# A Fourier mixing and low-rank mixer kernel: where batch 0's narrow sums run, when batch 1 is folded, and how its sine groups are formed

## The chip, the cores and the metric

The kernel runs on one core of one Trainium2 chip. The time is device microseconds of one launch; lower is better. The kernel before was timed three times: 446.45, 447.03 and 447.28 us, median 447.03 us. Five engines work side by side, each through its own queue in order: TensorE (PE; its weight loads are the row PEld), VectorE (DVE), ScalarE (ACT), GpSimd (POOL) and SyncE (SP, which here only issues DMAs).

## The reference

The input `x` is 8 batches of 3136 rows of 256 channels. Each batch goes through a two-dimensional Fourier transform, of which the real part is kept; then a low-rank mixing along the rows is added, and then a two-layer product over the channels.

```python
X = np.fft.fft(x, axis=1)
X = np.fft.fft(X, axis=2)
x = X.real.astype(np.float32)              # 8 x 3136 x 256

xt = x.transpose(0, 2, 1)
h = xt @ U @ V                             # rank 32, along the 3136 rows
u = x + h.transpose(0, 2, 1)
ch = np.maximum(u @ w_ch1, 0.0) @ w_ch2    # 256 -> 1024 -> 256
out = u + ch
```

## The kernel before

The Fourier transforms are matrix products with tables of sines and cosines (`tabs`: 0 is sine, 1 is cosine) that the kernel generates itself. Real input and the symmetry of sines and cosines let it work on folded data: rows n and S-n, channels d and D-d, and the two halves of the rows are added and subtracted first.

**Fold (`fold`, L402).** For a batch `b`, rows arrive in `xf` (forward) and `xr` (reversed), two halves `a` each. For each half VectorE folds along the channels (`along_d`, L382, instruction at L386, two parts for each of `xr` and `xf`), then combines forward and reversed rows (`mirror`, L394, into `EOS`); at the end `half` (L398) combines the two halves into `G[b % 2][par]`, the stationary operand of the transform. In batch 1, GpSimd copies channel 0 aside (`alone`, L390). `load_half` (L106) issues the loads of the next batch through GpSimd's queue. These are 16 steps for batch 1.

**Transform along the rows (`seq`, L470).** For each `par` (parity of the output), `typ` (1 cosine, 0 sine) and `pn` (parity of the row tile) there is a group of four products of 128 x 425 columns into one PSUM bank of the tag `dft`, of which there are three. The group with `pn == 0` is copied out by ScalarE (`ev`, L489); with `pn == 1`, VectorE forms the sum of both (`up`, L500) and their difference (`down`, L504) into the arrays `A` (cosine) and `B` (sine), and the small sum `TF` (L492) for the low-rank part. For some groups the `pn == 0` half is itself folded at the output: `halves` (L425) computes only the 229 columns from the middle on, in two parts, and VectorE forms the other columns from their difference (L436) and these from their sum (L437). `quarters` does the same twice, for the batches from `B0 = 2` on.

**The narrow row (`first_channel`, L614, through `narrow`, L545).** The first channels of batches 0 and 1 need a product of their own with 32 stationary columns: 16 small products into `ptc` (L556), a copy by ScalarE of one half of the partitions to `evc` (L560), and three operations for each parity on a few partitions: the small sum (L570), `up` (L573) and `down` (L574) into row R of `VA[b]`, the moving operand of the low-rank product. VectorE can read the other half of `ptc` in PSUM. Where `eng` is GpSimd, ScalarE also copies that half to `evo` (L563), and the sums read both from SBUF. Batch 1 and the later batches' shared narrow step use GpSimd; batch 0 uses VectorE. With `late` given, the two `down` operations are handed back and run later.

**Channels and the chunks.** `chan` (L628; `even_ch` and `odd_ch` for later batches) transforms pieces of `A` and `B` along the channels into `S` and `T`. The rows of all batches are then worked on in 49 chunks of 512 rows. `front(c)` (L712) forms a chunk's `u`: a low-rank product (L709) into PSUM, and VectorE's sum of it with `S` or `T` (L725). `first_product` (L729, product at L735) multiplies with `w_ch1`, ScalarE applies the maximum with 0 (L737); `second_product` (L739, product at L751) multiplies with `w_ch2`, and VectorE adds `u` (L757 to L760).

**What sets the order.** The setup, batch 0 and the first chunk are written in the order in which each engine's queue runs them (`tc.manual_schedule()`). At the start of chunk 1 (`c == 1`) `order.close()` ends that; from there on a planner orders the instructions by priority, which follows the program's order, and by its own estimate of when each is ready. Only those marked by `pin` keep the program's order. The loop of chunks has eight slots each (slot 8c + j). The dictionary `due` holds what else is issued in a slot; `spread(steps, lo, hi)` puts step n of N at slot `lo + (hi - lo) * n // N`:

```python
        for j in range(JT):
            if c < NCH:
                first_product(c, j)
            if c > 0 and j % 2 == 1:
                second_product(c - 1, j // 2)
            for step in due.get(8 * c + j, []):
                step()
            if j == 3 and c + 1 < NCH:
                front(c + 1)
```

So what is due in slot 3 stands ahead of `front(1)`, in slot 11 ahead of `front(2)` and in slot 19 ahead of `front(3)`. The pieces of batch 0's channels that are left are due in slots 2, 3, 8, 9, 10 and 11, behind the first two pieces and the late `down`s. Behind those, GpSimd's queue has its fills (`ta_rows(1)`, `column_zeros`, `ME`, `g_zeros(1)`, `va_zeros(1)`, L986 to L991), then what the fold issues.

Of the kernel before, what the change touches and what calls it, by code (L numbers as in the profile page):

```python
# [27 lines left out]
def kernel(  # L28
# [9 lines left out]
    nc = tc.nc  # L38
# [67 lines left out]
    def load_half(b, a):  # L106
        load_f(b, a)
        load_r(b, a)
        load_0(b, a, nc.gpsimd)
# [177 lines left out]
    def ktiles(par):  # L287
        return [i for i in range(NI) if (i + 1) % 2 == par]

    def kp(i):  # L290
        return KP if i == NI - 1 else PQ
# [90 lines left out]
    def along_d(a, src, dst, part):  # L382
        v = src[:, a, :, P:]
        lo, hi = (bass.AP(v.tensor, v.offset, [v.ap[0], v.ap[1], [s, 2], [2 * s, QD]])
                  for s in (-1, 1))
        pin(nc.vector.tensor_tensor(  # L386
            dst[:, a, :, part * P:(part + 1) * P].rearrange("p i (k t) -> p i k t", k=2), lo, hi,
            op=AL.subtract if part == 0 else AL.add))

    def alone(a, src, dst):  # L390

        pin(nc.gpsimd.tensor_copy(dst[:, a, :, 256:257], src[:, a, :, 0:1]))

    def mirror(a, cols, op):  # L394
        pin(nc.vector.tensor_tensor(EOS[:, a, :, cols], EOF_[:, a, :, cols],  # L395
                                    EOR_[:, a, ::-1][:, :, cols], op=op))

    def half(b, par, cols):  # L398
        pin(nc.vector.tensor_tensor(G[b % 2][par][:, :, cols], EOS[:, 0, :, cols],  # L399
                                    EOS[:, 1, :, cols], op=AL.add if par == 0 else AL.subtract))  # L400

    def fold(b):  # L402

        for a in range(2):
            for src, dst in ((xr, EOR_), (xf, EOF_)) if b == 1 else ((xf, EOF_), (xr, EOR_)):
                if b < B0:
                    yield lambda a=a, src=src, dst=dst: (alone(a, src, dst),
                                                         along_d(a, src, dst, 0))
                else:
                    yield lambda a=a, src=src, dst=dst: along_d(a, src, dst, 0)  # L410
                yield lambda a=a, src=src, dst=dst: along_d(a, src, dst, 1)
            if b + 1 < B:
                yield lambda a=a: load_half(b + 1, a)
            yield lambda a=a: mirror(a, slice(0, 128), AL.subtract)
            yield lambda a=a: mirror(a, slice(128, 258 if b < B0 else 256), AL.add)
        for par in range(2):
            yield lambda par=par: half(b, par, slice(0, 258 if b < B0 else 256))
# [48 lines left out]
    def join_t(eng):  # L466

        eng.tensor_tensor(TS, TF[:, :, 0], TF[:, :, 1], op=AL.add)  # L468

    def seq(b, par, typ, pn):  # L470

        if b not in ST:
            d = ST[b] = {}
            d["A"] = wp.tile([P, HALF + 1], BF16, tag="A", name="A", bufs=1)
            d["B"] = wp.tile([P, HALF + 1], BF16, tag="B", name="B", bufs=1)
            d["S"] = wp.tile([P, HALF + 1], BF16, tag="S", name="S", bufs=2)
            d["T"] = wp.tile([P, HALF + 1], BF16, tag="T", name="T", bufs=2)
        d = ST[b]
        g = G[b % 2][par]
        if pn == 0 and (b >= B0 or b == 1 and typ == 1):  # L480
            (quarters if b >= B0 else halves)(d, g, par, typ)
            return
        pt = psum.tile([P, QW], FP32, tag="dft", name="pt", bufs=3)
        for n, i in enumerate(ktiles(pn)):
            nc.tensor.matmul(pt[:], g[:kp(i), i, P * typ:P * (typ + 1)], tabs[typ][:kp(i), i, par, :],  # L485
                             start=(n == 0), stop=(n == NI // 2 - 1))
        if pn == 0:
            ev = d["ev"] = wp.tile([P, QW], FP32, tag="ev", name="ev", bufs=4)
            nc.scalar.copy(ev[:], pt[:])  # L489
            return  # L490
        ev = d["ev"]
        nc.vector.tensor_tensor(TF[:, typ, par], pt[:, NQ:QW], ev[:, NQ:QW], op=AL.add)  # L492
        if b == 0 and typ == 1 and par == 1:
            join_t(nc.vector)
        dst = d["A"] if typ == 1 else d["B"]
        if par == 0:
            up, c0 = dst[:, HALF // 2::-2], 0
        else:
            up, c0 = dst[:, HALF // 2 - 1:0:-2], 1
        nc.vector.tensor_tensor(up, pt[:, c0:NQ], ev[:, c0:NQ], op=AL.add)  # L500

        def down():
            dn = dst[:, HALF // 2 + 2 - par:HALF + 1 - par:2]
            nc.vector.tensor_tensor(dn, *((ev[:, 1:NQ], pt[:, 1:NQ]) if typ == 1 else  # L504
                                          (pt[:, 1:NQ], ev[:, 1:NQ])), op=AL.subtract)
        if b == 0 and typ == 1:
            return down
        down()

    B0 = 2  # L510
# [103 lines left out]
    def first_channel(b, **kw):  # L614
        dst = VA[b][R:R + 1]
        yield from narrow(1, lambda par, i: G[b][par][:kp(i), i, 256:256 + R], dst, TF[:1, 0],
                          None, **kw)
        mid = (HALF + S) // 2
        for lo, hi in ((HALF + 1, mid), (mid, S)):
            def turn_row(lo=lo, hi=hi):  # L620
                if b:
                    nc.gpsimd.tensor_copy(dst[:, lo:hi], dst[:, S - lo:S - hi:-1])
                    return
                with tc.issue_after(LAST[0].ins):
                    nc.scalar.copy(dst[:, lo:hi], dst[:, S - lo:S - hi:-1])
            yield turn_row

    def chan(b, lo, hi, h, tag=("dft", 3), dve=False):  # L628
        d = ST[b]
        pt = psum.tile([P, CH], FP32, tag=tag[0], name="pst", bufs=tag[1])  # L630
        nc.tensor.matmul(pt[:, :hi - lo], MC[:, h * P:(h + 1) * P], d["A"][:, lo:hi],  # L631
                         start=True, stop=False)
        nc.tensor.matmul(pt[:, :hi - lo], MSN[:, h * P:(h + 1) * P], d["B"][:, lo:hi],  # L633
                         start=False, stop=True)
        (nc.vector.tensor_copy if dve else nc.scalar.copy)(
            d["ST"[h]][:, lo:hi], pt[:, :hi - lo])
# [31 lines left out]
    def joined(b):  # L668

        join_t(nc.gpsimd)  # L670
        if b >= B0:
            nc.gpsimd.tensor_copy(TS[:1, 0], trow[:, (b - B0) * R:(b - B0 + 1) * R])
            nc.sync.dma_start(out=VA[b % 2][R:R + 1, :], in_=rows[b - B0:b - B0 + 1, :])
# [96 lines left out]
    def transform(b):  # L770

        for par in range(2):
            for typ in (1, 0):
                for pn in range(2):
                    yield lambda par=par, typ=typ, pn=pn: seq(b, par, typ, pn)
        if b < B0:
            row = list(first_channel(b, eng=nc.gpsimd))
            yield from row[:2]
            yield lambda: (row[2](), joined(b))
            for ch in range(4):  # L780
                for h in range(2):
                    yield lambda ch=ch, h=h: chan(b, ch * 392 + (1 if ch else 0),
                                                  (ch + 1) * 392 + 1, h)
            yield from row[3:]
            yield lambda: (lowrank(b), last_row(b))
            return
        for ch in range(4):
            yield lambda ch=ch: (even_ch(b, ch), across(b, ch, False))
            yield lambda ch=ch: (odd_ch(b, ch), across(b, ch, True), ch < 3 or joined(b))
        yield lambda: lowrank(b)  # L790
# [139 lines left out]
    MDT = [MSN, MC]  # L930
    keep_m(1, 0)
    seq(0, 0, 0, 0)
    fold_pe(1, 0, 1, False)
    keep_m(1, 1)
# [15 lines left out]
    nc.scalar.activation(MC[:], abm[:], AF.Sin, scale=TWO_PI / 2 ** 17, bias=c_nhp)  # L950
    nc.gpsimd.tensor_single_scalar(MC[0:1], MC[0:1], 0.5, op=AL.mult)
    late = []
    narrow_0 = list(first_channel(0, tag=("p2", 2), late=late))
    narrow_0[0]()
    seq(0, 0, 1, 0)
    for step in narrow_0[1:3]:
# [40 lines left out]
    def spread(steps, lo, hi):  # L997

        for n, step in enumerate(steps):
            due.setdefault(lo + (hi - lo) * n // len(steps), []).append(step)  # L1000

    for b in range(1, B):
        hi = 8 * (b * S // CH - 1) + 2
        if b == 1:
            spread(list(fold(b)), 4, 23)
            spread(list(transform(b)), 23, hi)
        else:
            spread(list(fold(b)), hi - 66, hi - 35)
            spread(list(transform(b)), hi - 33, hi)
        if b == B0:  # L1010
            for at, step in zip((24, 23, 21, 20, 19, 18, 12), column_steps()):
                due.setdefault(hi - at, []).append(step)
# [46 lines left out]
```

## Time and profile before

| | |
|---|---|
| Median of three runs | 447.03 us |
| The profiled execution's own time | 447.31 us |
| Span of its instructions | 445.2 us |
| PE busy | 435.7 us, 98% |
| DVE busy | 353.1 us, 79% |
| ACT busy | 297.5 us, 67% |
| POOL busy | 85.7 us, 19% |
| Granted TensorE clock | 1.00 |

The span runs from the first to the last profiled instruction; launch and end lie around it. A row of the order of time reads: start, duration, engine, line, operation, output and inputs, shapes, and how many instructions of one kind are merged (x2); in square brackets stands how long the engine sat idle before it, and what ended that. A row of the busy time by stretch reads: the stretch, its length, then the busy time with the number of instructions for PE, PEld, DVE, ACT and POOL, the granted clock, the share of the DMA engines and the GB/s moved. A row of a group ends in the total busy time, the mean duration in ns, and the idle time before the group's instructions. PE's records overlap, since products are pipelined: four products in a row end later than the sum of their starting distances. A few per cent of the product records are missing from the trace.

### The profile page before, as it was taken

The page shows a single profiled execution, that of the slowest core. Times are in us where ns is not written, and L with a number is a line of the kernel's source. Part 1 is how long each engine was busy: PE and PEld are TensorE (multiplying, and loading weights), DVE is VectorE, ACT ScalarE, POOL GpSimd, SP SyncE. Part 2 cuts the span into 40 slices and gives each one's busy share as a digit, 9 for nine tenths or more (in the row PEclk, how much of TensorE's full clock was granted, in tenths as well). Part 3 has the DMA queues.
Part 4 walks back from the last instruction along what each step waited for, and adds up shares of the span by engine and source line. Part 5 has one row for each costly group of instructions (what it writes and reads, how often), then busy time and mean ns, then how long its engine had stood idle before and what let it go on. Part 6 is the DMA issues. An engine that isn't in the chain of part 4 may idle for free.

```text
span 445.2 us, 8087 instructions
## 1 busy us (share of the span) xinstructions
PE 435.7 (98%) x2960; PEld 316.4 (71%) x3012; DVE 353.1 (79%) x838; ACT 297.5 (67%) x564; POOL 85.7 (19%) x144
## 2 busy tenths in 40 slices
PE   8999999999999999999999999999999999999997
PEld 6456766776677777777777777777777777777775
DVE  8879998888998799878998789878998776443433
ACT  8857747565885669655875569655876569656562
POOL 8973217300931002300211001300000000000000
PEclk9999999999999999999999999999999999999999
DMA  7998997995199437674779537782333332434343
GB/s 133 210 230 180 229 173 117 245 153 103 49 230 265 120 106 216 190 171 73 157 203 222 108 103 216 196 167 71 95 119 95 91 100 73 117 97 121 93 125 112
DMA packets 103249, 65.36 MB, mean 147 GB/s; under 512 B 73806, under 2 KB 99624, under 8 KB 100464
## 3 DMA queue, kind: packets, MB, share of 16 engines
q1 hardware_dynamic: 97528, 39.10, 40.1%
q0 software_dynamic: 5664, 25.75, 21.6%
q8 instruction: 23, 0.38, 0.3%
q14 instruction: 16, 0.13, 0.1%
q10 hardware_dynamic: 18, 0.00, 0.0%
HBM read 29.33 MB, written 25.69 MB: 124 GB/s over the span
## 4 chain that ended last, share of the span: by engine, by line
PE 91%; DVE 2%; DMA 2%; issue 1%; POOL 1%; ACT 1%; DVEq 0%; POOLq 0%
PE p L751 38%; PE p L735 35%; PE pt L485 6%; PE ph L709 5%; DMA xb<-in_x_dram,xidx 2%; PE ptq L446 2%; PE pst L643 1%; PE pst L652 1%; PE m L850 1%; PE ptc L556 1%; ACT h L737 0%; DVE eor L386 0%; PE pst L631 0%; DVE eof L386 0%; PE pst L633 0%
## 5 line engine op out<-in xcount | busy, mean ns | idle before, releaser
L737 ACT ACTIVATE h<-p 128x512 bf16<-128x512 f32 x392 | 222.0, 597 | 119.5 <-PE p L735 107.3
L735 PE MATMUL p<-u,w 128*128 128x512 bf16 x735 | 209.3, 379 | 1.2 <-DVE B L500 0.2
L751 PE MATMUL p<-w,h 128*128 128x256 bf16 x1568 | 203.0, 273 | 1.4
L751 PEld LDWEIGHTS <-h 128*128 128x128 bf16 x1568 | 153.2, 98 | 50.4 <-DVE o L760 0.3
L735 PEld LDWEIGHTS <-w 128*128 128x128 bf16 x784 | 106.1, 144 | 35.1 <-issue 2.0
L757 DVE TENSOR_TENSOR o<-p,ut 128x4 f32<-128x4 f32 (+1 forms) x100 | 16.2, 162 | 54.9 <-PE p L751 53.3
L759 DVE TENSOR_TENSOR o<-p,ut 128x254 f32<-128x254 f32 (+1 forms) x100 | 40.5, 405 | 0.0
L760 DVE TENSOR_TENSOR o<-p,ut 128x254 f32<-128x254 f32 (+1 forms) x100 | 40.5, 405 | 0.0
L468 POOL TENSOR_TENSOR tab<-tf 128x64 bf16<-128x64 f32 x7 | 3.1, 440 | 179.2 <-DVE tf L492 179.1
L386 DVE TENSOR_TENSOR eof<-xf 99x1024 bf16<-99x1024 f32 x28 | 35.8, 1293 | 0.0
L386 DVE TENSOR_TENSOR eor<-xr 99x1024 bf16<-99x1024 f32 x28 | 34.8, 1247 | 0.0
L725 DVE TENSOR_TENSOR u<-ph,S 128x512 bf16<-128x512 f32 (+23 forms) x63 | 34.3, 553 | 0.0
L725 DVE TENSOR_TENSOR u<-ph,T 128x512 bf16<-128x512 f32 (+23 forms) x63 | 34.2, 553 | 0.0
L55 POOL DMA_INDIRECT xf<-in_x_dram,xidx x14 | 17.3, 1234 | 62.0 <-DVE eof L386 48.5
L709 PE MATMUL ph<-va,ta 128*128 128x512 bf16 (+15 forms) x124 | 28.6, 328 | 0.3
L485 PEld LDWEIGHTS <-g 98*128 98x128 bf16 (+1 forms) x152 | 14.7, 98 | 13.1 <-issue 0.7
L395 DVE TENSOR_TENSOR eos<-eof,eor 99x1024 bf16<-99x1024 bf16 (+1 forms) x28 | 19.2, 702 | 0.0
L654 DVE TENSOR_TENSOR S<-evd,pst 128x392 bf16<-128x392 f32 (+1 forms) x24 | 13.5, 564 | 6.4 <-PE pst L652 4.1
L485 PE MATMUL pt<-tabs,g 98*128 98x425 bf16 x80 | 17.6, 344 | 0.0
L457 DVE TENSOR_TENSOR ev<-ptq,ex 128x131 f32<-128x131 f32 (+1 forms) x24 | 6.9, 289 | 12.9 <-ACT ex L450 12.9
L399 DVE TENSOR_TENSOR g<-eos 99x2048 bf16<-99x2048 bf16 (+1 forms) x14 | 16.9, 1217 | 0.0
L485 PE MATMUL pt<-tabc,g 98*128 98x425 bf16 x72 | 15.5, 344 | 0.0
(198 smaller groups left out, 381.0 us busy)
## 6 DMA issues: line engine op xcount, KB each, us to landing
out_dram<-o SPq DMA_DIRECT2D x48, 512.0 KB
xr<-in_x_dram POOLq DMA_DIRECT2D x14, 784.0 KB, 8.2
xb<-in_x_dram POOLq DMA_DIRECT2D x2, 392.0 KB, 7.9
ut<-u SPq DMA_TRANSPOSE x49
w<-in_moe_w_ch_dram POOLq DMA_DIRECT2D x1, 512.0 KB
out_dram<-o SPq DMA_DIRECT2D x4, 128.0 KB
va<-in_moe_V_dram POOLq DMA_DIRECT2D x2, 196.0 KB
w<-in_moe_w_ch_dram POOLq DMA_DIRECT2D x1, 256.0 KB, 7.2
```

The lines of the kernel that those rows point to most:

```text
L55: nc.gpsimd.indirect_dma_start(out_, None, bass.AP(t.tensor, t.offset, [[w, rows], [1, w]]), bass.IndirectOffsetOnAxis(idx, 0), element_of ...
L386: pin(nc.vector.tensor_tensor(dst[:, a, :, part * P:(part + 1) * P].rearrange("p i (k t) -> p i k t", k=2), lo, hi, op=AL.subtract if part ...
L395: pin(nc.vector.tensor_tensor(EOS[:, a, :, cols], EOF_[:, a, :, cols], EOR_[:, a, ::-1][:, :, cols], op=op))
L399: pin(nc.vector.tensor_tensor(G[b % 2][par][:, :, cols], EOS[:, 0, :, cols], EOS[:, 1, :, cols], op=AL.add if par == 0 else AL.subtract))
L485: nc.tensor.matmul(pt[:], g[:kp(i), i, P * typ:P * (typ + 1)], tabs[typ][:kp(i), i, par, :], start=(n == 0), stop=(n == NI // 2 - 1))
L709: nc.tensor.matmul(ph, TA[b % 2][:k, s * P:(s + 1) * P], VA[b % 2][:k, lo:hi], start=start, stop=True)
L725: nc.vector.tensor_tensor(u[:, s, col:col + hi - lo], ph[:, col:col + hi - lo], src, op=AL.add)
L735: nc.tensor.matmul(p1[:], W1[:, s, j::JT], k["u"][:, s, :], start=(s == 0), stop=(s == 1))
L737: LAST[0] = nc.scalar.activation(k["h"][:, j, :], p1[:], AF.Relu)
L751: nc.tensor.matmul(p2[:, t % w, :], h[:, j, rs], W2[:, j, :], start=(j == 0), stop=(j == JT - 1))
L759: nc.vector.tensor_tensor(o[:, ts, 1:P], p2[:, :w, 1:P], ut[:, ts, 1:P], op=AL.add)
L760: nc.vector.tensor_tensor(o[:, ts, P + 1:D], p2[:, :w, P + 1:D], ut[:, tT, P - 1:0:-1], op=AL.add)
```

## The change

The narrow sums of batch 0 are given to GpSimd; batch 1's fold is spread over slots 2 to 21 instead of 4 to 23, and its transform over 21 to 42 instead of 23 to 42; batch 1's sine groups with `pn == 0` go through `halves`, as its cosine groups do.

```diff
@@ seq
-        if pn == 0 and (b >= B0 or b == 1 and typ == 1):
+        if pn == 0 and b:
             (quarters if b >= B0 else halves)(d, g, par, typ)
             return
@@ setup
     late = []
-    narrow_0 = list(first_channel(0, tag=("p2", 2), late=late))
+    narrow_0 = list(first_channel(0, tag=("p2", 2), late=late, eng=nc.gpsimd))
     narrow_0[0]()
@@ the order of work
     for b in range(1, B):
         hi = 8 * (b * S // CH - 1) + 2
         if b == 1:
-            spread(list(fold(b)), 4, 23)
-            spread(list(transform(b)), 23, hi)
+            spread(list(fold(b)), 2, 21)
+            spread(list(transform(b)), 21, hi)
```

`hi` is 42 for batch 1. The functions that the new lines call are those above.

## The prediction

> **What bounds the kernel now.** I read the page first, then the busy time by stretch, then the order of time around the lines that the change touches.
>
> ```profile
> PE 435.7 (98%) x2960; PEld 316.4 (71%) x3012; DVE 353.1 (79%) x838; ACT 297.5 (67%) x564; POOL 85.7 (19%) x144
> PE 91%; DVE 2%; DMA 2%; issue 1%; POOL 1%; ACT 1%; DVEq 0%; POOLq 0%
> 40.00:50.00 10.00, 9.95 (x69) 7.32 (x69) 9.94 (x17) 7.66 (x14) 4.07 (x6) 1.00 0.90 203
> 50.00:60.00 10.00, 9.93 (x68) 6.79 (x68) 9.86 (x24) 5.36 (x11) 2.09 (x3) 1.00 1.08 230
> 60.00:70.00 10.00, 9.79 (x73) 6.45 (x73) 9.42 (x22) 5.07 (x10) 2.60 (x4) 1.00 0.74 161
> ```
>
> TensorE is busy 98% of the span and is 91% of the chain that ended last: a microsecond is won by giving it less to stream or by removing a wait of its own. In the rows by stretch (busy PE, PEld, DVE, ACT, POOL), VectorE is as full as TensorE from 40 to 60 us, which is where the change puts its work. So VectorE time is no gain by itself; it decides only when it makes TensorE wait.
>
> The first stage, in order of time, is another matter: there TensorE waits in a chain.
>
> ```profile
> 25.58 0.51 ACT L560 COPY evc<-ptc 64x425 f32<-64x425 f32 x1 [0.48 <-PE ptc L556]
> 26.12 0.18 DVE L570 TENSOR_TENSOR tf<-ptc,evc 1x32 f32<-1x32 f32 x1 [0.15 <-ACT evc L560]
> 26.17 0.19 POOL L224 MEMSET ta<- 128x128 int32 x1
> 26.40 0.52 ACT L489 COPY ev<-pt 128x425 f32<-128x425 f32 x1 [0.31 <-PE pt L485]
> 27.12 0.59 DVE L573 TENSOR_TENSOR va<-ptc,evc 1x392 bf16<-1x392 f32 x1
> 28.64 0.19 DVE L492 TENSOR_TENSOR tf<-pt,ev 128x32 f32<-128x32 f32 x1 [0.24 <-PE pt L485]
> 28.87 0.22 DVE L468 TENSOR_TENSOR tab<-tf 128x64 bf16<-128x64 f32 x1
> 29.58 0.36 ACT L680 CAST ta<-ptt 32x256 bf16<-32x256 f32 x1 [1.22 <-PE ptt L678]
> 29.65 0.75 POOL L194 MEMSET va<- 1x785 int32 x1
> 30.07 0.59 PE L709 MATMUL pu<-va,ta 65*128 65x512 bf16 x2
> ```
>
> The last group's sum (28.64) waited for TensorE, not for the narrow sums ahead of it on VectorE; from it run the join (28.87), the copy of TA (to 29.94) and the low-rank product (30.07).
>
> **The change, part by part.** *Narrow sums of batch 0.* VectorE loses four operations between 26.12 and 27.71 and, further on, the two `down` operations (L574):
>
> ```profile
> 31.66 1.06 DVE L504 TENSOR_TENSOR A<-ev,pt 128x392 bf16<-128x392 f32 x2
> 32.75 1.22 DVE L574 TENSOR_TENSOR va<-evc,ptc 1x392 bf16<-1x392 f32 x2
> 33.72 0.33 PE L633 MATMUL pst<-B,msn 128*128 128x392 bf16 x1
> 34.03 0.59 PE L709 MATMUL ph<-va,ta 65*128 65x512 bf16 x2
> 34.09 0.57 DVE L635 CAST T<-pst 128x392 bf16<-128x392 f32 x1
> 34.46 2.36 PE L735 MATMUL p<-u,w 128*128 128x512 bf16 x10
> 34.69 0.69 DVE L725 TENSOR_TENSOR u<-ph,S 128x512 bf16<-128x512 f32 x1
> 35.30 0.68 DVE L725 TENSOR_TENSOR u<-ph,T 128x512 bf16<-128x512 f32 x1
> 35.90 2.35 DVE L386 TENSOR_TENSOR eor<-xr 99x1024 bf16<-99x1024 f32 x2
> ```
>
> The first four win nothing: VectorE would stand idle before 28.64, which waits for TensorE. The two `down`s win a little. A 512-column product takes (2.36 - 0.38) / 9 = 0.22 us, so a 392-column one 0.17; after 33.72 the product of `front(1)` could start at 33.89 and started at 34.03, when the `down`s were out: **-0.14 us**. ScalarE gains a copy, and GpSimd the six sums. Their price on GpSimd is in batch 1's narrow step:
>
> ```profile
> 68.31 0.51 ACT L563 COPY evo<-ptc 64x425 f32<-64x425 f32 x1
> 68.91 0.49 POOL L570 TENSOR_TENSOR tf<-evo,evc 1x32 f32<-1x32 f32 x1 [5.41 <-ACT evo L563]
> 69.46 1.02 POOL L573 TENSOR_TENSOR va<-evo,evc 1x393 bf16<-1x393 f32 x1
> 70.44 1.47 POOL L574 TENSOR_TENSOR va<-evc,evo 1x392 bf16<-1x392 f32 x1
> 71.97 0.25 POOL L570 TENSOR_TENSOR tf<-evo,evc 1x32 f32<-1x32 f32 x1
> ```
>
> The extra copy ends at 26.09 + 0.51 = 26.60, pushes the next copy (26.40) by 0.2 us, and that is covered by the wait before 28.64. GpSimd starts at 26.69; with 0.55 us from sum to `up` and 0.98 from `up` to the next, the second sum ends at 28.71 (the join wants it by 28.87) and the second `up` at 29.79 (the low-rank product wants it when TA is out, 29.94). It just fits: **0**. With `up` at 1.47 it ends at 30.76, and the first chunk is 0.7 us late; with sums of 0.25 it has half a microsecond to spare. What waits behind the six sums on GpSimd are its fills (26.17 to 30.40, 4.2 us), which move to about 32 to 36, and then the fold's column copies. SP's loads of columns need one of the fills and are due from slot 8, after 36; the column copies have their first reader in the mirror step, here at 41.77 and with the fold's shift not before 39:
>
> ```profile
> 41.77 0.69 DVE L395 TENSOR_TENSOR eos<-eof,eor 99x1040 bf16<-99x1040 bf16 x1
> ```
>
> So this too costs 0; without that cover a late copy would hold VectorE's queue, and `u` with it, us for us.
>
> *Sine groups of batch 1.* Two groups go from four 425-column products to four of 229, for a copy of 229 columns and two VectorE operations more. Cosine groups do so already:
>
> ```profile
> L485 PE MATMUL pt<-tabs,g 98*128 98x425 bf16 x80 | 17.6, 344 | 0.0
> 55.74 0.89 PE L485 MATMUL pt<-tabs,g 98*128 98x425 bf16 x4
> 56.26 0.35 DVE L436 TENSOR_TENSOR ev<-pth,ev 128x196 f32<-128x196 f32 x1
> 57.15 0.19 DVE L492 TENSOR_TENSOR tf<-pt,ev 128x32 f32<-128x32 f32 x1
> ```
>
> Four products take 0.89 us with the last at 0.344, so (0.89 - 0.344) / 3 = 0.18 each; at 229 columns 0.10. Eight of them: **-0.64 us** of TensorE. VectorE pays 57.15 - 56.26 = 0.89 us a group, 1.8 us in all, against 1.22 taken away in the loop: 0.56 us more before `u` of chunk 4. The group's PSUM bank, one of three, is now held until VectorE's second operation instead of until a copy; TensorE's products for the chunks use other banks, so 0.
>
> *The fold.* A slot is one step of the chunk loop, eight to a chunk. The diff moves the fold by two slots, not the three of its description: 16 steps now start at slot 2, so two stand before `front(1)` (slot 3; none before), nine instead of seven before `front(2)` (slot 11), 16 instead of 14 before `front(3)` (slot 19). Its loads move with it, from slots 8 and 17 to 6 and 15, behind GpSimd's fills; they fetch batch 2, whose fold has slots from 24 on, so 0. The transform gets 21 slots for its 22 steps instead of 19 and ends where it did: 0.
>
> VectorE's order in chunk 0 is written out by hand. The first `along_d` (about 1.2 us, half of 2.35) takes the place of the `down`s, 32.75 to 33.97: free. The second follows the copy of T at 34.66 and pushes both halves of `u` by 2.35 / 2 = 1.17 us: S out at 36.55, T at 37.15. TensorE's first product on chunk 1 is the ninth of the ten at 34.46: 34.46 + 8 x 0.22 - 0.14 = 36.04 in the new kernel. In program order it waits 36.55 - 36.04 = 0.51, then 37.15 - 36.77 = 0.38: **0.89 us**. But from chunk 1 on a planner orders the work, and two channel pieces of 2 x 0.17 us each are ready: with them 0.89 - 0.68 = 0.21. I take the middle leaning to the pieces, **+0.45**.
>
> `front(3)` is the other place:
>
> ```profile
> 52.72 0.21 PEld L735 LDWEIGHTS <-w 128*128 128x128 bf16 x2 [0.29 <-DVE u L725]
> 53.24 2.37 DVE L399 TENSOR_TENSOR g<-eos 99x2064 bf16<-99x2064 bf16 x2
> 65.67 0.68 DVE L725 TENSOR_TENSOR u<-ph,S 128x512 bf16<-128x512 f32 x1
> 67.94 0.38 PE L735 MATMUL p<-u,w 128*128 128x512 bf16 x1 [0.21 <-DVE B L500]
> ```
>
> Here `u` was already 0.29 us late, with the two `half` operations (2.37) behind it. Now they come first by slot: `u` is 2.37 - 1.22 = 1.15 later. What hides it is chunk 2's second products, 32 x 0.11 = 3.5 us, ready by then: 0, or up to +1.15 where the planner misjudges. `u` of chunk 4 was out at 66.35 for a product at 67.94; now 66.91 for 67.16. Hidden, barely.
>
> **Sum**: -0.14 - 0.64 + 0.45 = -0.33. The profiled execution took 447.31 us around its span of 445.2; that gives 446.98, and 0.28 less against the median of 447.03: **446.7 us**.
>
> A rule against the change: the Trainium skill, GPSIMD Engine Reference, section 1, says GpSimd shares SBUF interfaces with VectorE and contends with VectorE operations with two SBUF inputs. These rows agree, 1.82 us for an operation that took 2.35 / 2 at 35.90:
>
> ```profile
> 73.62 1.02 POOL L574 TENSOR_TENSOR va<-evc,evo 1x392 bf16<-1x392 f32 x1
> 73.89 1.82 DVE L386 TENSOR_TENSOR eof<-xf 99x1024 bf16<-99x1024 f32 x1
> ```
>
> **Rivals.**
> - *Nothing waits* (26%). The planner hides both late `u`s, and the 0.29 goes: -0.14 - 0.64 - 0.29 = -1.07, 446.0. For it: TensorE hardly ever waits in the planned part. Against: VectorE is at 99%.
> - *The fold stands before `u`* (26%). VectorE runs fold steps ahead of `u` at slots 3 and 19 while TensorE's queue has the products of that `u` next: -0.78 + 0.89 + 1.15 = +1.26, 448.3: slower. It decides once the wait at slot 19 passes about 0.8. For it: the 0.29 above. Against: the second products as cover.
> - *GpSimd holds the first chunk* (8%): slow `up`s, +0.7, 447.4. Against: VectorE's sums beside them there read one operand from PSUM.
> - *GpSimd's fills slow the fold* (6%). Pushed to 32 to 36 us they lie beside the first two `along_d`, which read two operands from SBUF; both at 1.82 instead of 1.17 put `u` 1.3 us later: -0.33 + 1.3 = +0.97, 448.0. Against: the operations that ran beside the slow rows were sums and copies, not fills. This is the skill's rule at its worst.
>
> **How the numbers follow.** The forecast has 34%, with its own range of 446.2 to 447.6. 0.2% is 0.9 us, about what this kernel's measurement can tell from no change. Faster: the second case, 26%. Slower: the third and half of the last, 29%. The rest, 45%, lies within. From 445.5 (the best case and half a microsecond) to 448.6 all five prices are inside.
>
> **What would show it.** Right: products of pth on tabs at 229 columns, x8; `down`s on GpSimd before 33.9; 30.07 unmoved; `u` of chunk 1 out near 37.1, with pieces between TensorE's products at 36 to 37. Wrong: the low-rank product waiting for GpSimd; a TensorE wait over 0.8 us before chunk 3; an `along_d` near 35 at 1.8 us; a lead won by 40 us and lost by 70.

## The result, and the profile after

| | before | after |
|---|---|---|
| Median (6 runs each, side by side) | 447.02 us (446.45 to 447.73) | 458.71 us (458.41 to 459.23) |
| Ratio, 95% interval | | 1.0261 [1.0248, 1.0275] |
| Profiled execution / its span | 447.31 / 445.2 us | 458.79 / 457.0 us |

The change makes the kernel 11.7 us slower. The page of the kernel after, its line of busy time and its chain of waits by engine:

```profile
PE 437.5 (96%) x2959; PEld 317.6 (69%) x3012; DVE 350.7 (77%) x836; ACT 298.2 (65%) x565; POOL 93.4 (20%) x150
PE 84%; DVE 5%; POOL 4%; DMA 4%; issue 2%; ACT 0%; DVEq 0%; POOLq 0%
```

TensorE has 1.8 us more busy time, not 11.8, and its share of the chain falls from 91% to 84%. In its place stand VectorE with 5% and GpSimd and a DMA with 4% each, which had 2%, 1% and 2%. So a wait came in. The busy time by stretch shows where (columns as in the prediction: PE, PEld, DVE, ACT, POOL, then the granted TensorE clock):

```profile
30.00:40.00 10.00, 0.94 (x4) 0.38 (x4) 0.73 (x2) 0.29 (x1) 2.59 (x5) 0.56 0.43 111
40.00:50.00 10.00, 9.60 (x36) 4.79 (x35) 7.15 (x10) 6.32 (x14) 7.29 (x18) 0.76 0.14 27
50.00:60.00 10.00, 9.89 (x66) 7.32 (x67) 9.94 (x14) 7.22 (x15) 4.70 (x8) 1.00 0.90 176
```

From 30 to 40 us no engine is busy for more than 2.59 of the 10 us. The list of waits of that stretch names them (engine, line and tile that waited, what it waited for, us in total, times, longest):

```profile
ACT ta L680 <- PE ptt L678: 11.7, 1, 11.7
PEld L678 <- DVE tab L468: 11.0, 1, 11.0
POOL tf L570 <- DMA xf<-in_x_dram,xidx: 10.9, 1, 10.9
PE ptt L678 <- DVE tab L468: 10.5, 1, 10.5
DVE tab L468 <- POOL tf L570: 10.4, 1, 10.4
```

It is one chain, read from the third row on: GpSimd's first narrow sum waited for a DMA, VectorE's join (L468) for that sum, TensorE's product for the low-rank table (L678) for the join, ScalarE's copy of TA for the product. In order of time, the instructions of that chain, with GpSimd's gathers ahead of it:

```profile
17.97 1.02 POOL L55 DMA_INDIRECT xf<-in_x_dram,xidx  x1 [0.30 <-issue]
19.99 0.99 POOL L55 DMA_INDIRECT xf<-in_x_dram,xidx  x1 [0.30 <-issue]
25.36 0.87 POOL L951 TENSOR_SCALAR mc<-mc 1x256 bf16<-1x256 bf16 x1
25.69 0.51 ACT L563 COPY evo<-ptc 64x425 f32<-64x425 f32 x1
37.11 0.24 POOL L570 TENSOR_TENSOR tf<-evo,evc 1x32 f32<-1x32 f32 x1 [10.88 <-DMA xf<-in_x_dram,xidx]
37.42 1.01 POOL L573 TENSOR_TENSOR va<-evo,evc 1x393 bf16<-1x393 f32 x1
38.78 0.22 DVE L468 TENSOR_TENSOR tab<-tf 128x64 bf16<-128x64 f32 x1 [10.37 <-POOL tf L570]
39.06 0.39 PE L678 MATMUL ptt<-msn,tab 128*128 128x256 bf16 x1 [10.51 <-DVE tab L468]
39.96 2.08 POOL L574 TENSOR_TENSOR va<-evc,evo 1x392 bf16<-1x392 f32 x2
42.14 2.77 PE L735 MATMUL p<-u,w 128*128 128x512 bf16 x6
48.45 0.21 PEld L735 LDWEIGHTS <-w 128*128 128x128 bf16 x2 [0.69 <-DVE u L725]
```

GpSimd was free at 26.23 and both operands (`evc`, `evo`) were in SBUF by 26.20. It stood still for 10.88 us until a transfer had landed that the sum does not read: `xf`, the forward rows of batch 1, which GpSimd's own queue had issued at 17.97 and 19.99. The trace gives these two gathers' time to landing:

```profile
DMA to landing us min/median/max: 12.5/14.7/16.9
```

The second one landed at 19.99 + 16.9 = 36.9, and the sum started at 37.11. In the kernel before, the product for the low-rank table had waited 0.18 us, for the same join:

```profile
29.15 0.28 PE L678 MATMUL ptt<-msn,tab 128*128 128x256 bf16 x1 [0.18 <-DVE tab L468]
```

How the delay travels, from the first weight load of each chunk's first product and the end of the span:

| | before | after | later by |
|---|---|---|---|
| low-rank table (L678) | 29.15 | 39.06 | 9.91 |
| chunk 0 | 30.86 | 41.91 | 11.05 |
| chunk 1 | 35.97 | 48.45 | 12.48 |
| chunk 2 | 45.03 | 57.64 | 12.61 |
| chunk 5 | 76.89 | 88.36 | 11.47 |
| end of the span | 445.2 | 457.0 | 11.8 |

The wait itself is 9.9 us. Another 2.6 us come up to chunk 1, where `u` is late by 0.8 (48.46 and 49.05, below) and TensorE runs at a lower clock. Shorter stretches of the same view show that clock:

```profile
30.00:34.00 4.00, 0.00 (x0) 0.00 (x0) 0.00 (x0) 0.00 (x0) 0.00 (x0) 0.65 0.82 199
34.00:39.00 5.00, 0.00 (x0) 0.00 (x0) 0.22 (x2) 0.00 (x0) 1.67 (x4) 0.50 0.21 62
...
43.00:44.00 1.00, 1.00 (x4) 0.48 (x3) 1.00 (x3) 0.60 (x1) 0.84 (x7) 0.50 0.40 80
44.00:45.00 1.00, 1.00 (x5) 0.36 (x4) 0.93 (x1) 0.66 (x2) 0.94 (x3) 0.57 0.97 182
45.00:46.00 1.00, 1.00 (x7) 0.64 (x6) 0.00 (x0) 1.00 (x3) 0.96 (x2) 1.00 0.00 0
```

The granted clock is 0.50 at the end of the idle stretch and stays there until about 44.9 (0.57 is the mean of a slice that is 0.86 at 0.50 and the rest at 1.00), 5.8 us after work came back at 39.06. The six products at 42.14 took 2.77 us. Those six stand 0.43 us apart; 512-column products at the full clock stand 0.22 apart. Of the 12.6 us 1.1 are won back between chunk 2 and chunk 5, while batch 1 is transformed; the experiments below give the sine groups and the early fold as the reason. The end of the span is 11.8 us later, but what lies outside the span is 0.3 us shorter in the kernel after, so the two profiled executions differ by 11.5.

### The profile page after: what moved, and what is told of

The parts are those of the page before. It is cut to its first block, busy times and chain, and to the rows that moved or that the text cites. A ratio compares the mean times of both kernels' runs of the same rounds, so it can differ in the third digit from the quotient of the medians.

```text
span 457.0 us, 8093 instructions
## 1 busy us (share of the span) xinstructions
PE 437.5 (96%) x2959; PEld 317.6 (69%) x3012; DVE 350.7 (77%) x836; ACT 298.2 (65%) x565; POOL 93.4 (20%) x150
## 4 chain that ended last, share of the span: by engine, by line
PE 84%; DVE 5%; POOL 4%; DMA 4%; issue 2%; ACT 0%; DVEq 0%; POOLq 0%
PE p L751 36%; PE p L735 33%; PE pt L485 5%; PE ph L709 4%; DMA xf<-in_x_dram,xidx 4%; PE ptq L446 2%; DVE eof L386 1%; PE pst L643 1%; DVE u L725 1%; PE pst L652 1%; DVE eor L386 1%; DVE g L399 1%; PE pst L631 0%; PE pst L633 0%; PE ptt L678 0%
## 5 line engine op out<-in xcount | busy, mean ns | idle before, releaser
L735 PE MATMUL p<-u,w 128*128 128x512 bf16 x734 | 211.9, 381 | 1.8 <-DVE u L725 0.4
L735 PEld LDWEIGHTS <-w 128*128 128x128 bf16 x784 | 106.2, 144 | 35.5 <-issue 2.0
L468 POOL TENSOR_TENSOR tab<-tf 128x64 bf16<-128x64 f32 x7 | 3.0, 422 | 177.9 <-DVE tf L492 177.8
L386 DVE TENSOR_TENSOR eof<-xf 99x1024 bf16<-99x1024 f32 x28 | 34.6, 1252 | 0.0
L725 DVE TENSOR_TENSOR u<-ph,S 128x512 bf16<-128x512 f32 (+23 forms) x63 | 34.4, 556 | 0.0
L725 DVE TENSOR_TENSOR u<-ph,T 128x512 bf16<-128x512 f32 (+23 forms) x63 | 34.4, 556 | 0.0
L55 POOL DMA_INDIRECT xf<-in_x_dram,xidx x14 | 18.6, 1325 | 67.1 <-DVE eof L386 50.0
L395 DVE TENSOR_TENSOR eos<-eof,eor 99x1024 bf16<-99x1024 bf16 (+1 forms) x28 | 18.6, 687 | 0.0
L485 PE MATMUL pt<-tabs,g 98*128 98x425 bf16 x72 | 15.8, 344 | 0.1
```

The lines of the kernel that those rows point to most:

```text
L55: nc.gpsimd.indirect_dma_start(out_, None, bass.AP(t.tensor, t.offset, [[w, rows], [1, w]]), bass.IndirectOffsetOnAxis(idx, 0), element_of ...
L386: pin(nc.vector.tensor_tensor(dst[:, a, :, part * P:(part + 1) * P].rearrange("p i (k t) -> p i k t", k=2), lo, hi, op=AL.subtract if part ...
L725: nc.vector.tensor_tensor(u[:, s, col:col + hi - lo], ph[:, col:col + hi - lo], src, op=AL.add)
L735: nc.tensor.matmul(p1[:], W1[:, s, j::JT], k["u"][:, s, :], start=(s == 0), stop=(s == 1))
```

## Experiments

Each kernel was timed beside the kernel before on the same chip. Where an edit is a part of the change, its lines are those of the diff above.

### The narrow sums alone

```diff
-    narrow_0 = list(first_channel(0, tag=("p2", 2), late=late))
+    narrow_0 = list(first_channel(0, tag=("p2", 2), late=late, eng=nc.gpsimd))
```

> Only the narrow sums of batch 0 go to GpSimd; fold and sine groups stay as before. Theory G (GpSimd's first sum waits until the gathered loads of batch 1, issued ahead of it on GpSimd's queue, have landed, about 36.9 us): nearly the whole loss is here, 457.5 to 459.5 us, with GpSimd idle some 10 us before its first small sum and TensorE idle about as long before the low-rank product of batch 0. Rival V (fold steps ahead of u on VectorE, with the sine groups' extra operations): this kernel is within 1 us of before, 446 to 448. Rival S (GpSimd's sums themselves are slow or collide with VectorE): some 448 to 450, with sums well over 1.5 us each.

459.21 us (458.79 to 460.0), ratio 1.0274 [1.0258, 1.029]. One argument holds the whole loss, and the same row carries it:

```profile
37.63 0.24 POOL L570 TENSOR_TENSOR tf<-evo,evc 1x32 f32<-1x32 f32 x1 [11.48 <-DMA xf<-in_x_dram,xidx]
```

### The other two parts without it

```diff
-        if pn == 0 and (b >= B0 or b == 1 and typ == 1):
+        if pn == 0 and b:
...
-            spread(list(fold(b)), 4, 23)
-            spread(list(transform(b)), 23, hi)
+            spread(list(fold(b)), 2, 21)
+            spread(list(transform(b)), 21, hi)
```

> The earlier fold and the sine groups folded at the output, with the narrow sums left on VectorE. Theory G: the long wait is gone, 446.2 to 448.8 us: 0.64 us less for TensorE, against a wait of about 0.9 us for u of chunk 1, which two along_d operations push back. Rival V: most of the loss stays, 455 us or more. Rival S: as theory G.

447.68 us (447.37 to 448.25), ratio 1.0016 [1.0007, 1.0025]. There is no stall of 10 us; what is left is the fold's push of `u` of chunk 1, here at full size (in order of time):

```profile
33.74 1.23 DVE L386 TENSOR_TENSOR eor<-xr 99x1024 bf16<-99x1024 f32 x1
...
36.61 0.68 DVE L725 TENSOR_TENSOR u<-ph,S 128x512 bf16<-128x512 f32 x1
...
37.35 0.44 PE L735 MATMUL p<-u,w 128*128 128x512 bf16 x1 [1.27 <-DVE u L725]
```

With the `down`s still on VectorE the first `along_d` starts only behind them, at 33.74, and both `along_d` stand ahead of `u`.

### Why GpSimd waits: the partition that is read

The sums read `evc` and `evo` at partition 64 and 96. In the kernel before, GpSimd's sums into `es` came right behind the same gathers and did not wait; they read 99 partitions, from 0 on. Nor did a fill that writes 64 partitions from 64 on (L226):

```profile
19.86 1.07 POOL L55 DMA_INDIRECT xf<-in_x_dram,xidx  x1 [0.30 <-issue]
21.14 0.40 POOL L879 TENSOR_TENSOR es<-xb 99x8 bf16<-99x8 bf16 x2
26.76 0.10 POOL L226 MEMSET ta<- 64x1 bf16 x1
```

The question is whether the start partition decides. Two kernels add one sum of eight elements to the kernel before, at the place where the narrow sums would go, on a table that is no longer read (the narrow sums stay on VectorE). One reads partition 64, as shown; the other has `0:1` in place of `64:65`:

```diff
+    nc.gpsimd.tensor_tensor(ncol[64:65], ncol[64:65], ncol[64:65], op=AL.add)
     late = []
```

> The kernel before with one small GpSimd sum more (8 elements of partition 64 of a tile that is no longer needed, into itself) where the narrow sums would go; the narrow sums stay on VectorE. Theory G: GpSimd sits idle about 10 us before it, to the landing of the last gather near 37 us, though nothing that it reads comes from a load; the time stays within 1.5 us of before, since only fills stand behind it. If the wait is one of the narrow sums' own data: no such idle time, the sum runs at about 26.3 us.

> As the run with one small GpSimd sum at partition 64, but at partition 0: the same 8 elements of the same tile, the same place in GpSimd's queue. Theory G in the form that the partition decides: no idle time for a load before it, the sum at about 26.3 us, and the time of the kernel before, 446.5 to 447.6 us. If any GpSimd sum waits for the gathers: again some 11 us idle and about 449 us.

GpSimd's rows, of partition 64 first:

```profile
37.98 0.36 POOL L952 TENSOR_TENSOR ncol<-ncol 1x8 f32<-1x8 f32 x1 [11.78 <-DMA xf<-in_x_dram,xidx]
...
43.96 0.70 DVE L395 TENSOR_TENSOR eos<-eof,eor 99x1040 bf16<-99x1040 bf16 x1 [1.97 <-POOL eof L392]
```

And of partition 0:

```profile
26.16 0.19 POOL L952 TENSOR_TENSOR ncol<-ncol 1x8 f32<-1x8 f32 x1
```

The same instruction at the same place waits 11.78 us at partition 64 and not at all at partition 0. The wait is put into the program when the kernel is built; the engine does not come to it by itself. The trace has semaphore instructions of the same line (L952) ahead of the sum at partition 64, which wait, among others, for the two semaphores that the two gathers raise when they land; ahead of the sum at partition 0 it has none. The kernel after has the same ones ahead of its first narrow sum (L570). So in these kernels a GpSimd sum whose input starts at partition 64 is made to wait for the gathers that are outstanding on GpSimd's queue, and one whose input starts at 0 is not. Why it is made so, and what holds for other start partitions, the runs do not say. The small sum writes to the partition that it reads; that the input decides and not the output follows from the fill above and from the kernel with row copies below, whose sums write to partition 32 and do not wait.

At partition 0 the time is 446.91 us, ratio 0.9994 [0.9985, 1.0003]. At partition 64 it was 449.32 in one run; the idle time is as expected, the time is 2.3 us up where at most 1.5 was expected. The last row says why: GpSimd's fills and column copies came late, and VectorE's mirror step (L395) waited 1.97 us for the last column copy, with `u` queued behind it. It is the loss that the prediction named for the case that the cover of the fills is gone.

### The dose: one gather issued later

The change whole, but the second gather issued only behind the narrow sums:

```diff
     def load_second(a):
         load_r(1, a)
-        load_f(1, a)
+        if a == 0:
+            load_f(1, a)
...
+    load_f(1, 1)
     ta_rows(1)
```

> The changed kernel whole, but the second of batch 1's two gathers is issued behind the narrow sums on GpSimd's queue instead of ahead of them; the first stays. Theory G: the first sum starts when the first gather lands, about 30.5 to 31 us instead of 37.1, so some 6 us come back: 450 to 453.5 us (the slow clock after the long wait goes too). Rivals V and S: no more than 1 us from the changed kernel, 458 to 460, since neither the fold's order nor the sums change.

452.13 us (451.9 to 452.81), ratio 1.0121 [1.0105, 1.0136]:

```profile
30.24 0.24 POOL L570 TENSOR_TENSOR tf<-evo,evc 1x32 f32<-1x32 f32 x1 [4.67 <-DMA xf<-in_x_dram,xidx]
```

With one gather outstanding GpSimd waits 4.67 instead of 10.88 us and the kernel loses 5.1 instead of 11.7. The wait follows the landing (17.96 + 12.0 = 30.0), and the time follows the wait. One expectation failed: the slow clock did not go. It was 0.50 from about 31.0 to 37.9 us, and it is part of the 5.1 us, since the low-rank table is only 3.0 us late (32.19).

### The change whole, read from partition 0

ScalarE copies the four rows to partition 0 (four copies of one row of 425; the room is a spare part of `G[1]`), and GpSimd reads them there. The output stays in row R of `VA`, the order of all else is that of the change.

```diff
+        def row_copies(par):
+            for k, pn in (("re", 0), ("ro", 1)):
+                spare = G[1][par][0:1].rearrange("p i w -> p (i w)").bitcast(FP32)
+                t[k, par] = spare[:, pn * QW:(pn + 1) * QW]
+                at = (2 * pn + par) * R
+                nc.scalar.copy(t[k, par], t["pt"][at:at + 1])
...
```

Calls of `row_copies` in `products` and `sums` take the place of the two copies to `evc` and `evo`. What stands behind the added lines is 15 lines further down in this kernel: L585 is L570, L588 is L573, L693 is L678, L740 is L725 and L750 is L735.

> The changed kernel whole, but ScalarE copies each of the four rows that the narrow sums of batch 0 need to partition 0 (two copies of one partition more), so that GpSimd reads from partition 0; loads and gathers are untouched. Theory G, in the form that the wait belongs to GpSimd operations that read from another partition than 0: no wait for the gathers, first small sum near 27 us, 446.0 to 448.5 us. Theory G in the form that any sum on GpSimd waits for the gathers: 458 us as the changed kernel. Rival V: 457 or more. Rival S: 448 to 450.

447.14 us (446.69 to 447.7), ratio 1.0001 [0.9992, 1.001]:

```profile
26.86 0.24 POOL L585 TENSOR_TENSOR tf<-g 1x32 f32<-1x32 f32 x1 [0.61 <-ACT g L574]
28.76 1.00 POOL L588 TENSOR_TENSOR va<-g 1x392 bf16<-1x392 f32 x1
29.23 0.62 DVE L468 TENSOR_TENSOR tab<-tf 128x64 bf16<-128x64 f32 x1
29.91 0.28 PE L693 MATMUL ptt<-msn,tab 128*128 128x256 bf16 x1 [0.76 <-DVE tab L468]
35.09 1.89 PE L750 MATMUL p<-u,w 128*128 128x512 bf16 x8
37.21 0.44 PE L750 MATMUL p<-u,w 128*128 128x512 bf16 x1 [0.23 <-DVE u L740]
37.80 0.38 PE L750 MATMUL p<-u,w 128*128 128x512 bf16 x1 [0.16 <-DVE u L740]
```

The loss of 11.7 us is gone once the sums read from partition 0, though the same six sums run on GpSimd. The low-rank table starts at 29.91 instead of 29.15: its wait grew from the 0.18 of the kernel before to 0.76. Part of that is the join, which took 0.62 us in the middle of GpSimd's `up` (28.76 to 29.76) where it took 0.22 in both other kernels. In the kernel after it lay beside an `up` as well, but there it began first (38.78, the `up` at 38.83). Chunk 1's first product could start 8 x 0.216 after 35.09, at 36.82, and started at 37.21; the second started 0.59 instead of 0.22 after it: 0.39 + 0.37 = 0.76 us of wait for `u`.

### Each part by itself

Five more kernels complete the table of the three edits; where the narrow sums are on GpSimd in it, they are read from partition 0 as above. Their edits are the lines shown: the condition on `pn == 0` (sine), the two `spread` calls (fold), the row copies (narrow sums).

> Only the sine groups of batch 1 are folded at the output. By the sum in the prediction: 0.64 us less for TensorE and VectorE's 1.8 us more hidden: 446.1 to 446.9 us. Rival V (VectorE is the bound between 40 and 67 us): the 1.8 us come out as TensorE's waits, 447.5 to 449.

> Only the fold and the transform of batch 1 start two slots sooner. Two along_d operations stand ahead of u of chunk 1, and the two down operations are still on VectorE as well: u comes 2.3 us later and TensorE waits 1.3 to 1.9 us for it: 448.0 to 448.9 us. Rival (the planner fills the wait): 446.8 to 447.4.

> The narrow sums on GpSimd from rows at partition 0 and the sine groups, with the fold at its old slots. No wait for the gathers; the low-rank product waits about 0.6 us longer than before (0.93 against 0.34, as with the rows at partition 0 and the early fold); no wait for u of chunk 1: 446.4 to 447.2 us. If the early fold's wait for u was hidden anyway, as with it: 447.1.

> The narrow sums of batch 0 on GpSimd from rows at partition 0, and nothing else of the change. Without the wait for the gathers the move itself costs what the later join costs and wins what the down operations cost TensorE: 0.6 - 0.14 us against before, 447.2 to 447.8 us.

> The row copies and the fold at slot 2, the sine groups as before: the pair that is still missing. If the fold's price hangs on VectorE's two down operations standing ahead of it (theory: with them gone the first along_d is free and only the second pushes u of chunk 1, by about 0.8 us of which part is given back): u of chunk 1 waits 0.7 to 0.8 us as in the kernel with all three edits, not 1.7, and the time is 447.0 to 448.0 us (rows alone took 447.6). If the fold costs its 1.3 us whatever stands ahead of it: 448.7 to 449.2 us.

| narrow sums | sine | fold | median, us | against before, us | ratio, interval | chunk 0 to 2, us | chunk 2 to 5, us |
|---|---|---|---|---|---|---|---|
| VectorE (before) | no | no | 447.00 to 447.05 | | | 14.18 | 31.85 |
| VectorE | yes | no | 446.79 | -0.26 | 0.9998 [0.9989, 1.0007] | 14.18 | 31.65 |
| VectorE | no | yes | 448.40 | +1.35 | 1.0035 [1.0022, 1.0049] | 15.94 | 31.43 |
| VectorE | yes | yes | 447.68 | +0.68 | 1.0016 [1.0007, 1.0025] | 15.93 | 30.73 |
| GpSimd, partition 0 | no | no | 447.59 | +0.59 | 1.0011 [1.0002, 1.002] | 14.04 | 31.86 |
| GpSimd, partition 0 | yes | no | 447.38 | +0.33 | 1.0010 [1.0001, 1.0019] | 14.04 | 31.64 |
| GpSimd, partition 0 | no | yes | 447.87 | +0.83 | 1.0029 [1.0014, 1.0043] | 14.77 | 31.42 |
| GpSimd, partition 0 | yes | yes | 447.14 | +0.14 | 1.0001 [0.9992, 1.001] | 14.78 | 30.73 |

The fifth column is the difference of two medians from the same chip. In the row with the fold and no sine groups on GpSimd three of the twelve runs took 449.5 to 451.0 us, so its median is the least firm. The last two columns are taken from one trace each: the time between the first weight loads of the first products of two chunks. Rows with and without one edit give its price. **Sine:** -0.26, -0.67, -0.26 and -0.69, on the mean -0.47 us. **Fold:** +1.35 and +0.94 with the `down`s on VectorE, +0.24 and -0.19 with them on GpSimd. **Narrow sums without the wait:** +0.59 and +0.59 without the fold, -0.52 and -0.54 with it. An interval is some 0.4 us to each side, so a single difference is not firm; that the fold is cheaper where the `down`s have left VectorE shows in both pairs.

The traces part these prices more finely. Up to chunk 2 the `down`s that leave VectorE win 0.14 us, and the fold costs 1.76 us with them on VectorE and 0.73 without. From chunk 2 to chunk 5, where batch 1 is transformed, the sine groups win 0.2 us with the fold at its old slots and 0.7 with the fold early; the early fold gives 0.43 back there without them and 0.9 with them. So the two edits help each other, and the mean of -0.47 stands for neither case. Why they do, the runs do not show. The trace of the fold alone shows the wait up to chunk 1:

```profile
33.73 1.23 DVE L386 TENSOR_TENSOR eor<-xr 99x1024 bf16<-99x1024 f32 x1
34.18 1.89 PE L735 MATMUL p<-u,w 128*128 128x512 bf16 x8
37.35 0.44 PE L735 MATMUL p<-u,w 128*128 128x512 bf16 x1 [1.27 <-DVE u L725]
37.94 0.38 PE L735 MATMUL p<-u,w 128*128 128x512 bf16 x1 [0.15 <-DVE u L725]
```

By the same reckoning as above, TensorE waits 37.35 - 35.91 = 1.44, then 0.37: 1.81 us against 0.76. Chunk 1 starts only 0.14 us later than with the rows at partition 0 (37.21), but there TensorE itself came 0.91 later to it, since the low-rank table was late.

The rows with the fold came out within what was expected for a price that hangs on the `down`s (447.0 to 448.0). The rows with the sine groups were expected at 446.4 to 447.2 and missed it with 447.38. The longer wait for the low-rank table (0.76 us) had been counted; the 0.64 us of the sine groups had been counted too, and without the early fold they win only 0.2. No kernel of the table is clearly faster than the kernel before.

## Why the prediction was wrong, step by step

- **What bounds the kernel** was right: TensorE, and in the first stage a chain of waits. The loss came in just that chain.
- **The narrow sums at "It just fits: 0"** is the step that failed. It let GpSimd start at 26.69, as soon as its own queue and the copies were done, and bounded the cost by 0.7 us. It weighed the sums' prices and forgot what else the instruction could wait for. Measured: start at 37.11, low-rank table 9.9 us late. The gathers were in the trace of before, on the same queue, 5 us ahead of the new place; but while they were under way no GpSimd operation there had an input that starts at partition 64. Batch 1's narrow step, from which the prices came, ran at 68.9, long after these two had landed. Yet a sign of the wait lay right there: another gather, issued at 61.93, took 6.6 us to land, to 68.5, and the step's first sum began at 68.91. ScalarE's copy of `evo` ended at 68.82, so the view put the idle time down to the copy. In the kernel after, the same step's wait is put down to the gather (the first row is of before, the second of after):

```profile
61.93 1.01 POOL L55 DMA_INDIRECT xf<-in_x_dram,xidx  x1 [8.91 <-DVE ev L436]
81.86 0.30 POOL L570 TENSOR_TENSOR tf<-evo,evc 1x32 f32<-1x32 f32 x1 [5.18 <-DMA xf<-in_x_dram,xidx]
```

- The sums' **prices** themselves were right: 0.24 and 1.01 us (0.25 and 1.02 said), 2.08 for both `down`s. "GpSimd holds the first chunk" had the place, with another mechanism and 0.7 us.
- **"It just fits" without the wait** was optimistic too: read from partition 0, with two copies on ScalarE for each parity in place of two in all, the narrow sums alone cost 0.59 us, near that rival's 0.7. The row copies are part of that price, so it is not shown what the sums would cost without both them and the wait. The **-0.14** of the `down`s was right: 14.04 against 14.18 us from chunk 0 to chunk 2.
- **Sine groups, -0.64**: the products of pth on tabs came with 229 columns, x8 (259 to 265 ns each, at 66.6 to 71.6 us). The sign was right. The size was right beside the early fold (0.7 us from chunk 2 to chunk 5) and too large without it (0.2).

```profile
L430 PE MATMUL pth<-tabs,g x8: 259/262/265, 66.6 to 71.6; 98*128 98x229 bf16 x6, 99*128 99x229 bf16 x2
```

- **The fold, +0.45**: the mechanism was right, the choice within it not. In program order it said 0.89 us, and with the planner's pieces in between 0.21. The planner put none there. In the kernel after, the eight products at 46.32 let the ninth start at 48.05; it started at 48.46, and the next 0.59 behind it: 0.41 + 0.37 = 0.78 us. That the first `along_d` is free because it takes the place of the `down`s holds: with them still on VectorE the wait is 1.81. What the sum left out is that the early fold gives time back from chunk 2 on, so that with rows at partition 0 its price was +0.24 or -0.19 us. (By its own figures the ninth product was due at 36.08 and not at 36.04, and the wait in program order 0.85; nothing hangs on it.)

```profile
46.32 1.89 PE L735 MATMUL p<-u,w 128*128 128x512 bf16 x8
46.57 1.23 DVE L386 TENSOR_TENSOR eor<-xr 99x1024 bf16<-99x1024 f32 x1
48.46 0.44 PE L735 MATMUL p<-u,w 128*128 128x512 bf16 x1 [0.25 <-DVE u L725]
49.05 0.38 PE L735 MATMUL p<-u,w 128*128 128x512 bf16 x1 [0.16 <-DVE u L725]
```

- **"GpSimd's fills slow the fold"** did not happen. Fills lay beside the first `along_d` (the longest at 44.27), and it took 1.22 us, where the two of the kernel before took 2.35 / 2 = 1.17 each. The Trainium skill, GPSIMD Engine Reference, section 1, has GpSimd contend with VectorE operations that have two SBUF inputs; for fills these rows do not show it, while the join's 0.62 us for 0.22 in the middle of a sum with two inputs agrees.

```profile
43.71 1.22 DVE L386 TENSOR_TENSOR eor<-xr 99x1024 bf16<-99x1024 f32 x1
44.27 1.40 POOL L193 MEMSET va<- 32x1568 int32 x1
```

- **The rest of the sum** came near: with the wait taken away the whole change is +0.14 us, ratio 1.0001 [0.9992, 1.001], against the -0.33 of the sum. That is in part luck, since the dearer move of the sums and the cheaper fold offset each other. The failed term alone put the result outside the range.

## What to carry to other kernels

An instruction that moves to another engine's queue also takes on what that queue has under way: before calling an idle engine free, list the transfers that it has issued and not yet seen land, and look in the trace for an operation of the same form, partitions included, that ran while such transfers were out. If there is none, the bound of its cost is their landing, not its own duration. A view names only the wait that ended last; two that end within half a microsecond of each other, as in batch 1's narrow step, look like one. In a kernel built like this one, where GpSimd has gathers outstanding, let its sums read from partition 0. Issuing a gather behind the sums shortened the wait too; issuing both there was not tried.

## What the hardware showed beside this

A wait of 10.5 us on TensorE costs more than itself. The last product before it ended at 28.56. The granted clock has a mean of 0.65 from 30 to 34 us, so it fell from 1.00 to 0.50 at about 31.2, some 2.6 us into the wait, and it was back at 1.00 at about 44.9, 5.8 us after work had come back. With one gather issued later it was 0.50 from about 31.0 to 37.9 us, 5.7 us beyond the return of work at 32.19. The Trainium skill, TensorE: Matmul & The Clock Gate, Part 1, has half the clock after an idle window of about 3.4 us and the full one after about as long a busy one, the window running freely. The half clock agrees, and so do the lengths: 13.7 and 6.8 us are four and two such windows, by an estimate from that figure, and work came back inside the last but one each time. The fall came after 2.6 us and so did not wait for a whole idle window.
